# Forgetting attention and a bilinear feed-forward on one core: the first third of a literal instruction order replaced

## The chip, the core and the metric

The program runs on one NeuronCore of a Trainium2 chip. The core has a matrix engine (PE, whose weight loads are shown apart as PEld), three engines for elementwise work (DVE, ACT, POOL), and SP, which here only issues transfers. Each engine works through its own queue in order. Matrix products land in PSUM, and one of DVE or ACT has to bring them to SBUF. The metric is the device time of one execution in microseconds.

## The reference

Inputs q, k, v are [8 batches, 8 heads, 576, 64] and f is [8, 8, 576], all 32-bit floats.

```python
scores = scale * np.matmul(q, k.transpose(0, 1, 3, 2))          # scale = 1/8
cum = np.cumsum(np.log(np.clip(f, 0.0001, 1.0)), axis=-1)
decay = cum[:, :, :, None] - cum[:, :, None, :]
scores = np.where(causal, -1000000000.0, scores + decay)
attn = np.exp(scores - np.max(scores, axis=-1, keepdims=True))
attn = attn / (np.sum(attn, axis=-1, keepdims=True) + 1e-09)
x = np.matmul(attn, v)                  # then heads side by side: x is [4608, 512]
return (x @ w_a) * (x @ w_b) @ w_out    # 512 -> 1536 -> 512
```

## The kernel before

**Attention.** The 64 heads are taken in 32 pairs t = 0 to 31; four pairs make one batch (t = 4*b + pr). A pair's 576 queries are cut in five blocks i = 0 to 4 of 128 rows (the last has 64), and causality cuts the keys of each. For a block PE makes the scores from the transposed q and k (tiles `qT`, `kT`, line 550; `sc` in PSUM), DVE takes the row maximum (line 645), ACT the exponential (lines 704 and 700), DVE the reciprocal of the row sum (line 714), and POOL or ACT multiplies it in (lines 725 and 723). The weights P (tiles `PA` for blocks 0 to 2, `PB` for 3 and 4) are transposed, in the first eight pairs mostly by PE against an identity (`psP`, brought back by lines 288 to 292), later by a transposing transfer that SP issues (line 739). PE multiplies them with v (line 768, `pv` and `pvx`), and DVE writes the result, transposed, to `xT0` to `xT3`, one tile for each place of a pair in its batch. For the first two batches PE adds the decay inside the score product (`crow`, `pick`, and the causal mask by `neg`, `low`); from the third on DVE adds it from a tile `spread` that a transfer or a PE product (`scd`) fills.

**Start.** Batch 0's q and k are loaded and cast to 16 bits by transfers that POOL issues (line 333), since POOL's queue is the one that can cast; the halves beyond the first go to the space of `wout`, which is free then. POOL also builds the identity (two instructions from masks.py). PE transposes q and k against it (`psT`, line 358), and DVE or ACT evicts them to `qT` and `kT`. In the places where PE would stand idle at the start, 24 operations "wake" make products that nobody reads (line 74, tile `wake`, four matmuls each).

**Feed-forward.** It runs on token chunks of 256, 256, 256, 384, four times 512, 384, and the last 1024 tokens in a form with fewer products. Of a chunk, PE makes `psa` = x@w_a and `psb` = x@w_b for 128 columns of the 1536 at a time, ACT or DVE casts `psa` to `a` (line 288), DVE multiplies `psb` by it (line 1072, `ht`), and `pso` is the product with w_out. The matmuls of all of these go through one helper, line 74. The first chunk needs rows 0 to 255 of batch 0 in all four `xT` tiles, that is, blocks 0 and 1 of pairs 0 to 3.

**What sets the order.** The program records 2480 operations, each with a number, its engine or the engines it may run on, and what it depends on. At the end `laid_out` reads three literal texts: ORDER is the sequence of the operation numbers, in which they are then written out (each engine's queue keeps it), CHOICE gives the engine for those that have a choice (D for DVE, A for ACT, P for POOL), and SLOTS says for each buffer ring which of its places each tile takes. PSUM has a ring of two for scores (`sc`, two banks each) and a ring of four (`ff`) for everything else; f32 loads share three places (`n32`).

```python
n_of = [x.split("-") for x in ORDER.split()]
seq = [ops[n] for x in n_of for n in range(int(x[0]), int(x[-1]) + 1)]
for o in ops:
    o.eng = names[next(letters)] if len(o.durs) > 1 else next(iter(o.durs))
...
for o in order:
    o.fn(o.eng)
```

The function of the kernel is one long function, of which the changed tables and their reader are a part:

Of the kernel before, what the change touches and what calls it, by code (L numbers as in the profile page):

```python
# [25 lines left out]
def kernel(  # L26
# [13 lines left out]
    B, H, S, D = q.shape  # L40
# [22 lines left out]
    qd = [perm.tile([128, 128], FP16, tag=f"qd{i}", name=f"qd{i}") for i in range(2)]  # L63
# [41 lines left out]
    def paddings():  # L105
# [14 lines left out]
    nv = [perm.tile([128, NSB, H, D], FP16, tag=f"nv{i}", name=f"nv{i}") for i in range(2)]  # L120
# [21 lines left out]
        PA:012302310231023102310231023102310231;PB:01101010101010101010101010101010;S:0101101001101001101010110  # L142
        0110101010101001010101010101010010011010100101001000100010011011010011010100110101001101010110101010101
        ;a16:0120120120120120120120120120120121021021201201201201021021020210210120120121021021021021021;bc:012
        0120120120120120120120120120;ff:01230123013200031230120131312313102312022101012133203012301230123012301
        2301302132021021230230201230231021301230123012012302131231231021230130230132103120301010312013210321023
        1023023102310321321302130213013210321032103102132132012312312303021021023103120313201302130230123120312
        0302102012120102301310210213023123201321301321320120320312032130213021302301213021303210312303021021320
        130213201302312031203120321032102301;ht:0123456789abcd0123456789abcd0123456789ab01cd2345678a019b23cd456
        8017a29bd345c0168279a34bd015c2;n16:01101001011000101001010101010101;n32:0120102102102102010202121220120  # L150
        110102121101202201201201202120;nv:0101010101;osb:010101010100101010101010101001;qd:01010101010101010101
        0101;sc:01010101010101010101010110100101011000101010110010010101101010101011010101010101010100101011101
        10010101011001010111010101010101010101010101010101;st:01234510324510324510324510324510
# [1404 lines left out]
    for n in cuts:  # L1558
# [5 lines left out]
        0 1 29 30 46 2 52 62 5 3 31 37 32 38 33-36 39 40 42 41 53 47 58 4 43 267 262 279 6-9 54 48 10 56 50 44  # L1564
# [161 lines left out]
```

## Time and profile before

| what | value |
|---|---|
| median of three runs | 394.4 us (393.54 to 395.13) |
| profiled execution, its own time | 396.1 us |
| its span from the first to the last instruction | 394.4 us |
| mean granted PE clock | 0.999 |
| PE busy | 381.1 us, 97% of the span |
| DVE busy | 329.1 us, 83% |
| ACT busy | 299.4 us, 76% |
| POOL busy | 281.0 us, 71% |
| first feed-forward product | at 35.80 us |

The span is what one execution shows from its first instruction to its last; its own time is 1.7 us longer, which lies around the span. That the span equals the median of the three runs is chance. In rows of the timeline the first number is the start in us, the second the time that the row's instructions take together, "x16" their count; "[0.30 <-DVE kT L292]" behind a row says that the engine stood idle for 0.30 us ahead of it, and what released it. Matmuls overlap, so two rows' starts tell more of a duration than the second number does.

### The profile page before, as it was taken

How to read it: one execution, taken by the hardware profiler on the slowest of the kernel's cores; microseconds unless marked ns; L12 is line 12 of the kernel's file. 1: busy time of each engine (PE TensorE's matmuls, PEld its weight loads, DVE VectorE, ACT ScalarE, POOL GpSimd, SP SyncE). 2: the span in 40 equal slices, each digit the busy share in tenths (PEclk: the TensorE clock that was granted, in tenths of full speed). 3: DMA queues.
4: the chain of work that ended last, by engine and by line, in shares of the span. 5: the costliest groups of instructions: out<-in, count | busy, mean ns of one | idle time of the engine just before them, and what ended most of it. 6: DMA issues, size and time to landing. Idle time of an engine off the chain costs nothing.

```text
span 394.4 us, 14909 instructions
## 1 busy us (share of the span) xinstructions
PE 381.1 (97%) x5816; PEld 253.9 (64%) x5816; DVE 329.1 (83%) x1035; ACT 299.4 (76%) x826; POOL 281.0 (71%) x482
## 2 busy tenths in 40 slices
PE   7899999999998999999899999999999999999996
PEld 3557887968765665655555655555555667666796
DVE  7888898998996888788788888757898899987992
ACT  4998999999886878868888588779899672556331
POOL 8689686768867689874899769578976891267600
PEclk9999999999999999999999999999999999999999
DMA  7999999999999999999998999999998898100005
GB/s 121 251 202 170 144 154 223 228 278 275 208 222 215 220 282 247 281 187 277 260 237 255 262 207 229 206 244 263 226 226 195 169 182 178 55 1 2 2 2 214
DMA packets 147190, 76.88 MB, mean 195 GB/s; under 512 B 124336, under 2 KB 128176, under 8 KB 147120
## 3 DMA queue, kind: packets, MB, share of 16 engines
q1 hardware_dynamic: 132824, 68.79, 77.9%
q0 software_dynamic: 14256, 7.08, 14.7%
q8 instruction: 45, 0.74, 0.8%
q14 instruction: 25, 0.20, 0.2%
q10 hardware_dynamic: 40, 0.07, 0.1%
HBM read 52.05 MB, written 9.58 MB: 156 GB/s over the span
## 4 chain that ended last, share of the span: by engine, by line
PE 73%; DMA 11%; DVE 5%; POOL 4%; ACT 3%; issue 2%; ACTq 0%; DVEq 0%; POOLq 0%
PE psa L74 15%; PE psb L74 15%; PE pso L74 13%; PE wg L74 5%; DMA PTA<-PA 5%; PE wb L74 4%; PE sc L550 3%; PE og L74 3%; DMA PTB<-PB 3%; PE pvx L768 3%; PE psT L358 2%; DVE S L673 2%; DMA wb<-in_moe_w_b_dram 2%; POOL PA L725 2%; PE wake L74 2%
## 5 line engine op out<-in xcount | busy, mean ns | idle before, releaser
L673 DVE CUSTOM_DVE_ANT_0 S<-sc,spread 64x576 f32<-64x576 f32 (+4 forms) x232 | 125.5, 561 | 14.5 <-ACT PA L704 4.8
L725 POOL TENSOR_SCALAR PA<-PA,st 128x256 f16<-128x256 f16 (+2 forms) x180 | 85.0, 481 | 9.6 <-DVE st L714 6.0
L74 PE MATMUL psb<-xT,wb 128*64 128x512 f16 (+2 forms) x864 | 88.7, 332 | 0.4 <-DVE ht L1072 0.2
L704 ACT ACTIVATE PA<-S,st 128x256 f16<-128x256 f32 (+2 forms) x168 | 84.1, 503 | 6.4 <-DVE st L673 5.8
L74 PE MATMUL psa<-xT,wa 128*64 128x512 f16 (+2 forms) x864 | 88.9, 333 | 0.0
L74 PE MATMUL pso<-wout,ht 128*64 128x512 f16 x672 | 81.8, 381 | 0.0
L725 POOL TENSOR_SCALAR PB<-PB,st 128x512 f16<-128x512 f16 (+1 forms) x90 | 63.6, 713 | 25.3 <-DVE st L714 8.8
L74 PEld LDWEIGHTS <-wb 128*64 128x64 f16 x960 | 55.9, 110 | 24.9 <-issue 1.8
L74 PEld LDWEIGHTS <-wa 128*64 128x64 f16 x960 | 55.2, 110 | 24.7 <-issue 2.2
L1072 DVE TENSOR_TENSOR ht<-psb,a 128x512 f16<-128x512 f32 (+1 forms) x90 | 57.5, 648 | 7.2 <-PE psb L74 5.1
L288 ACT CAST a<-psa 128x512 f16<-128x512 f32 (+1 forms) x90 | 49.4, 550 | 18.0 <-PE psa L74 15.8
L74 PEld LDWEIGHTS <-ht 128*64 128x64 f16 x696 | 38.3, 110 | 26.8 <-issue 2.2
L704 ACT ACTIVATE PB<-S,st 128x512 f16<-128x512 f32 x56 | 40.2, 720 | 3.2 <-DVE st L673 2.7
L704 ACT ACTIVATION_READ_ACCUMULATOR PA<-S,st 128x1 f32 x168 | 32.1, 191 | 0.0
L630 POOL TENSOR_SCALAR_AFFINE_SELECT spread<-spread 128x768 f32<-128x768 f32 x24 | 20.8, 866 | 14.0 <-DMA spread<-cum_d 13.9
L700 ACT ACTIVATE PB<-S,st 128x576 f16<-128x576 f32 x28 | 21.7, 776 | 10.7 <-DMA PTB<-PB 4.1
L768 PEld LDWEIGHTS <-nv 128*64 128x64 f16 x640 | 21.8, 110 | 8.5 <-DMA PTA<-PA 2.3
L673 DVE CUSTOM_DVE_ANT_1 S<-sc,spread 128x256 f32<-128x256 f32 x48 | 19.7, 419 | 7.5 <-ACT PB L704 1.6
L1273 POOL TENSOR_TENSOR hy<-wu 128x512 f16<-128x512 f32 x9 | 11.6, 1302 | 19.7 <-DVE wu L1273 19.6
L714 DVE RECIPROCAL st<-st 128x2 f32<-128x2 f32 x128 | 18.1, 156 | 7.2 <-ACT PA L704 3.6
L673 DVE DVE_READ_ACCUMULATOR2_ANT st<- 128x1 f32 (+1 forms) x280 | 22.8, 81 | 0.0
L550 PE MATMUL sc<-kT,qT 64*128 64x512 f16 (+4 forms) x144 | 21.0, 326 | 1.2 <-ACT kT L288 0.4
(156 smaller groups left out, 692.8 us busy)
## 6 DMA issues: line engine op xcount, KB each, us to landing
spread<-cum_d SPq DMA_DIRECT2D x24, 576.0 KB, 6.4
q<-in_q_dram SPq DMA_DIRECT2D x14, 576.0 KB, 5.3
k<-in_k_dram SPq DMA_DIRECT2D x14, 576.0 KB, 5.4
out_dram<-osb SPq DMA_DIRECT2D x29, 256.0 KB, 4.0
v<-in_v_dram SPq DMA_DIRECT2D x24, 256.0 KB, 5.8
wout<-in_moe_w_out_dram POOLq DMA_DIRECT2D x3, 512.0 KB, 8.0
nv<-in_v_dram POOLq DMA_DIRECT2D x8, 128.0 KB, 5.1
wa<-in_moe_w_a_dram POOLq DMA_DIRECT2D x2, 512.0 KB, 7.5
```

What stands on the lines that cost most here:

```text
L74: nc.tensor.matmul(out=out[r], lhsT=lhsT[:, r], rhs=rhs, **kw)
L288: nc.scalar.copy(out=out_, in_=in_)
L550: nc.tensor.matmul(out=dst, lhsT=lhsT, rhs=rhs, start=start, stop=stop, skip_group_check=True)
L630: nc.gpsimd.affine_select(out=c[:, :, 0:SM].rearrange("p h (j k) -> p h j k", k=128), in_=c[:, :, SM:2 * SM].rearrange("p h (j k) -> p h j ...
L673: nc.vector.tensor_tensor_reduce(out=o, in0=x, in1=y, scale=-1.0, scalar=3e38, op0=ADD, op1=MIN, accum_out=m)
L700: nc.scalar.activation(out=p_blocks(t, 4), in_=T[("s" if direct else "z", t, 4)], func=EXP, bias=st[:, 8:9], scale=sign, accum_out=st[:, 1 ...
L704: nc.scalar.activation(out=p_blocks(t, i)[:, :, h, :], in_=(T[("s", t, i)][:, h, :] if direct else T[("z", t, i)][:, h * n:h * n + n]).rea ...
L714: nc.vector.reciprocal(out=st[:, 20 + 2 * i:22 + 2 * i], in_=st[:, 10 + 2 * i:12 + 2 * i])
L725: VEC[e].tensor_scalar(out=p, in0=p, scalar1=st[:, c:c + 1], scalar2=1.0, op0=MUL, op1=MUL)
L768: nc.tensor.matmul(out=o[HP[h], 128 * i:128 * i + 128], lhsT=vt[:, j, pr + NP * h, :], rhs=pt[:, base_blk[i] + 2 * block_at(t, i, j) + h, ...
L1072: nc.vector.tensor_tensor(out=ht[:, 0:n_], in0=T.pop(("psb", t0, fbs))[:, 0:n_], in1=T.pop(("a16", t0, fbs))[:, 0:n_], op=MUL)
L1273: VEC[e].tensor_tensor(out=out_, in0=x, in1=y, op=op)
```

## The change

Only the three texts change; the code that records the operations, and each operation, is the same. The last 1720 operations of ORDER are the same in the same sequence; the first 760 are arranged anew, and 45 operations get another engine. SLOTS is written anew to suit.

```diff
     SLOTS = """
-        PA:012302310231023102310231023102310231;PB:01101010101010101010101010101010;S:0101101001101001101010110
+        PA:012330123012301230123012301230123012;PB:01101010101010101010101010101010;S:0101010110100101100101010
...
     ORDER = """
-        0 1 29 30 46 2 52 62 5 3 31 37 32 38 33-36 39 40 42 41 53 47 58 4 43 267 262 279 6-9 54 48 10 56 50 44
+        2 5-10 519 11 12 52 53 3 0 1 29 30 13 31 32 54 37 38 55 46 47 33 34 39 62 48 58 43 56 57 36 50 49 51 35
...
     CHOICE = """
-        DDDDADADADAAPPAPPPAPPAADAPPPPPPAPADDDDPPPAPPPPPDDDDPAAPAPPPADDDADAADAAAADDPPPAPAPPPADDAAPPAPPAPAADADAAA
+        DDPDAAAADDDAPPPAPPAPPDDADPPAPPPAPPDDDDAPAPPPPPPDDDDPPAPAPPPPDDADDAAAAAAADDPPPPPPPPADDDDAPPAPAPPPDDAAPPP
```

On PE the heads that differ have the same 184 operations in another sequence; behind them, from a score product of pair 11 on (line 538, at 109.75 us in the trace of before), PE's sequence is the same. DVE gets one operation more in its head (232 for 231), POOL three more (137 for 134), ACT four fewer (173 for 177).

On PE all 24 wakes stand ahead of the first `psa` before and after. Of the work that stood ahead of it, three transposes of P (block 2 of pairs 0, 2 and 3, six matrices each) and the score products of blocks 3 and 4 of pair 2 now stand behind it, and one `scd` product from behind it stands ahead. The score products of blocks 0 and 1 of pair 2 and 3 stood behind those of block 2 of pair 0, and pair 3's also behind block 2 of pairs 1 and 2; now those of all four pairs stand ahead of the first product of a block 2. The order of SP begins with a load of the last 64 rows of batch 2's v, ahead of the load of f.

POOL from its start, before (a tile's number is its place in the program's count; `k16` and `q16` are the first halves of batch 0's k and q, `wout16` the place of the second halves):

```order
L333 DMA k16_130<-in_k_dram 64x2x576
masks.py:197 MEMSET ident16_70 128x128
masks.py:199 ISA
masks.py:199 AFFINE_SELECT ident16_70<-ident16_70 128x128
L333 DMA q16_136<-in_q_dram 64x2x576
L333 DMA wout16_78<-in_q_dram 128x2x576
L333 DMA q16_136<-in_q_dram 64x2x576
L333 DMA k16_130<-in_k_dram 64x2x576
L333 DMA wout16_78<-in_k_dram 128x2x576
```

and after:

```order
masks.py:197 MEMSET ident16_70 128x128
masks.py:199 ISA
masks.py:199 AFFINE_SELECT ident16_70<-ident16_70 128x128
L333 DMA q16_170<-in_q_dram 64x2x576 x2
L333 DMA k16_239<-in_k_dram 64x2x576 x2
L333 DMA wout16_78<-in_q_dram 128x2x576
L333 DMA wout16_78<-in_k_dram 128x2x576
```

The identity moves ahead of the first load of k, and both parts of q ahead of k.

DVE from the first row maxima on, before (`st` is a pair's small tile of maxima and sums, `sc0` holds the scores of blocks 0 and 1, `sc1` of block 2, `sc2` of block 3, `sc3` of block 4):

```order
L645 TENSOR_REDUCE st_384<-sc0_301 128x2 x2
L645 TENSOR_REDUCE st_384<-sc1_337 128x2
L290 TENSOR_SCALAR qT_253<-psT_318 128x576
L292 COPY kT_255<-psT_356 128x576
L714 RECIPROCAL st_384<-st_384 128x2
L645 TENSOR_REDUCE st_458<-sc0_403 128x2 x2
L714 RECIPROCAL st_384<-st_384 128x2
L292 COPY kT_255<-psT_421 128x576
L645 TENSOR_REDUCE st_545<-sc0_479 128x2 x2
```

and after:

```order
L645 TENSOR_REDUCE st_371<-sc0_315 128x2 x2
L645 TENSOR_REDUCE st_425<-sc0_334 128x2 x2
L290 TENSOR_SCALAR qT_268<-psT_374 128x576
L714 RECIPROCAL st_371<-st_371 128x2
L292 COPY kT_272<-psT_435 128x576
L714 RECIPROCAL st_371<-st_371 128x2
L292 COPY kT_272<-psT_436 128x576
L645 TENSOR_REDUCE st_512<-sc0_491 128x2 x2
L292 COPY spread0_84<-scd_508 128x512
L645 TENSOR_REDUCE st_554<-sc0_524 128x2 x2
```

Pair 1's first maxima now follow pair 0's at once, and pair 3's are the last row; before, pair 3's stood eight rows below the last one printed, behind two more maxima of block 2 (one of them is in the second row printed).

DVE up to the last eviction that the first `psa` needs, before:

```order
L292 CAST xT2_74<-pv_786 128x256
L645 TENSOR_REDUCE st_458<-sc2_814 128x2
L292 CAST xT0_72<-pv_737 128x256
L645 TENSOR_REDUCE st_458<-sc3_823 128x1
L292 CAST xT1_73<-pv_873 128x256
L292 COPY xT3_75<-psP_855 128x768
L292 COPY xT3_75<-psP_903 128x768
L292 CAST xT3_75<-pv_922 128x256
```

and after:

```order
L292 CAST xT0_72<-pv_708 128x256
L292 CAST xT1_73<-pv_745 128x256
L714 RECIPROCAL st_554<-st_554 128x2
L292 COPY xT3_75<-psP_726 128x768
L292 COPY spread1_85<-scd_742 128x512
L645 TENSOR_REDUCE st_371<-sc2_755 128x2
L292 CAST xT3_75<-pv_781 128x256
L714 RECIPROCAL st_425<-st_425 128x2
L714 RECIPROCAL st_371<-st_371 128x2
L645 TENSOR_REDUCE st_371<-sc3_764 128x1
L292 COPY xT2_74<-psP_801 128x768
L292 CAST xT2_74<-pv_843 128x256
```

The four casts from `pv` are the evictions in question; the last one is pair 3's before and pair 2's after, and of the larger maxima (`sc2`, `sc3`) those of pair 0 stand ahead of it now, where before those of pairs 0 and 1 did.

74 lines of the change are left out of this document (45 added, 29 removed), and 168 rows, old and new, of the table ORDER.

## The prediction

> **What bounds the kernel now.** I read the page first (span, busy times, the chain that ended last), then busy times by stage, then PE's timeline up to the first feed-forward product.
>
> ```profile
> span 394.4 us, 14909 instructions
> PE 381.1 (97%) x5816; PEld 253.9 (64%) x5816; DVE 329.1 (83%) x1035; ACT 299.4 (76%) x826; POOL 281.0 (71%) x482
> PE 73%; DMA 11%; DVE 5%; POOL 4%; ACT 3%; issue 2%; ACTq 0%; DVEq 0%; POOLq 0%
> ```
>
> PE is busy for 97% of the span and carries 73% of the chain. The same by stage (after the two times: the stretch's length, then busy time of PE, PEld, DVE, ACT, POOL, and the granted clock):
>
> ```profile
> 2.80:35.80 33.00, 30.98 (x544) 18.14 (x545) 27.90 (x68) 27.43 (x83) 27.95 (x55) 1.00 1.07 203
> 35.80:109.75 73.95, 73.59 (x1534) 60.23 (x1529) 67.34 (x237) 69.49 (x192) 56.63 (x93) 1.00 1.15 213
> 109.75:130.00 20.25, 18.28 (x266) 12.40 (x262) 16.59 (x62) 15.84 (x50) 14.84 (x28) 1.00 1.11 234
> ```
>
> 35.80 is the first feed-forward product, 109.75 the score product from which PE's sequence is the same in both orders. Between the two PE is unbusy for 0.36 us. So whatever PE work is moved from ahead of 35.80 to behind it is paid there in full, since no idle time waits to take it in. Where the 33 us ahead of the first product go:
>
> ```profile
> 2.80 4.48 PE L74 MATMUL wake<-ident 128*64 128x512 f16 x20 [2.80 <-POOL ident masks.py:199]
> 7.21 0.69 PE L358 MATMUL psT<-ident,q 64*64 64x64 f16 x18
> 7.71 0.66 PE L358 MATMUL psT<-ident,k 64*64 64x64 f16 x18
> 8.30 1.06 PE L74 MATMUL wake<-ident 128*64 128x512 f16 x8
> 9.29 0.48 PE L358 MATMUL psT<-ident,wout 64*64 64x64 f16 x36
> 9.70 0.34 PE L550 MATMUL sc<-kT,qT 64*128 64x256 f16 x4
> 20.27 0.34 PE L550 MATMUL sc<-kT,qT 64*128 64x256 f16 x4
> 32.70 0.53 PE L74 MATMUL psP<-ident,PA 128*64 128x128 f16 x12 [0.16 <-POOL PA L725]
> 33.06 0.60 PE L74 MATMUL wake<-ident 128*64 128x512 f16 x4
> 34.06 0.41 PE L74 MATMUL scd<-crow,pick 128*64 128x512 f16 x2
> 34.27 0.36 PE L768 MATMUL pv<-xT,nv 128*64 128x128 f16 x6
> 34.56 0.39 PE L550 MATMUL sc<-kT,qT 64*128 64x512 f16 x2
> 35.80 1.06 PE L74 MATMUL psa<-xT,wa 128*64 128x256 f16 x16
> 109.75 0.51 PE L538 MATMUL sc<-kT,qT 64*128 64x128 f16 x10
> ```
>
> PE starts at 2.80. Ahead of 109.75 it is unbusy for 2.80 + 2.02 + 0.36 = 5.18 us altogether, and since its set of operations there does not change, that total (and what slow matmuls at the start may give) bounds what a new order can gain by 109.75. PE looks busy, but part of it is wakes, whose products nobody reads. The useful chain is elsewhere: first scores of pair 0 at 9.70, of pair 3 only at 20.27, then maxima, exponentials, norms, transposes, and the products with v, whose evictions by DVE release 35.80. DVE, with 27.90 busy of 33.00, is the densest engine of that chain.
>
> **The change, part by part.** *1. Start.* Now the identity stands ahead of the loads in POOL's queue.
>
> ```profile
> 1.33 0.83 POOL L333 DMA_DIRECT2D k<-in_k_dram  x1 [0.81 <-POOLq L1710]
> 2.46 0.29 POOL masks.py:199 TENSOR_SCALAR_AFFINE_SELECT ident<-ident 128x128 f16<-128x128 f16 x1
> ```
>
> The load that stood ahead goes behind: 2.15 − 1.33 = 0.82 us (the next instruction began at 2.15), so the identity ends at 2.75 − 0.82 = 1.93 and PE starts at 1.98. The k load itself now stands third, behind both q loads; its transposes come late enough on PE to cover that (nine wakes stand ahead now, five before). If that cover is short, the price is one or two issues of 0.83. PE's row is then five wakes at the first row's price, 4.48; four more at 0.99 a pair (8.30 to 9.29), 2.0; four groups of transposes at 0.50 (7.21 to 7.71), 2.0; two wakes, 0.5 to 1.0. Pair 0's first scores: 1.98 + 4.48 + 2.0 + 2.0 + 0.7 = 11.2, against 9.70, thus 1.5 later. Pair 1's follow at once.
>
> The first 20 wake matmuls took 0.224 us each, the next eight 0.124 (0.99 / 8). The Trainium skill, "TensorE: Matmul & The Clock Gate", section "What's actually happening", says that the array runs at half rate until about 3.4 us of sustained activity, a span of time in a free-running window and not a number of matmuls. By that rule an earlier start ends the slow phase earlier, perhaps inside the fifth wake, an estimate of up to 0.8 us less or more at 11.2; the trace agrees that there is a slow phase and cannot show what sets its end.
>
> *2. DVE's chain to the last eviction.*
>
> ```profile
> 10.36 1.89 DVE L645 TENSOR_REDUCE st<-sc 128x2 f32<-128x512 f32 x3 [0.61 <-PE sc L550]
> 20.93 1.02 DVE L645 TENSOR_REDUCE st<-sc 128x2 f32<-128x512 f32 x2
> 17.20 0.68 DVE L292 COPY spread<-scd 128x512 f32<-128x512 f32 x1
> 25.20 0.74 DVE L292 COPY kT<-psT 128x576 f16<-128x576 f16 x1
> 25.92 1.20 DVE L645 TENSOR_REDUCE st<-sc 128x2 f32<-128x1024 f32 x1
> 27.77 1.04 DVE L292 COPY xT<-psP 128x768 f16<-128x768 f16 x2
> 34.76 0.41 DVE L292 CAST xT<-pv 128x256 f16<-128x256 f32 x1
> ```
>
> A maximum starts 0.66 behind its scores (9.70 to 10.36): 11.8 now. From there to the end of pair 3's first maxima the new order has four double maxima (1.02 each), three evictions of q or k (0.74), one copy (0.68) and two reciprocals (some 0.3): 4.1 + 2.2 + 0.7 + 0.3 = 7.3, thus 19.1, against 20.93 + 1.02 = 21.95. Behind it and up to the last of the four evictions the new order has nine reciprocals (0.8), three copies to spread (2.0), four maxima of block 2 (3.8, taken at 0.96, between the 1.02 and 1.20 of the rows shown), one kT (0.7), four copies from psP (2.1), one maximum over 1024 (1.2), one over 576 (0.7), four casts (1.6): 13.0, thus 32.1 without waits. Before, the same stretch took 35.17 − 21.95 = 13.2 with waits in it. I take 32.4 for the first psa, against 35.80: **−3.4**. Ends: −4.0 (no wait and a shorter slow phase) to −1.4 (the waits of about 2 us that DVE had there come again).
>
> *3. What PE owes.* Three transposes of P, 0.36 each (32.70 to 33.06), and the score products of blocks 3 and 4 of pair 2, 1.24 (34.56 to 35.80), go behind the first psa; one scd, 0.21 (34.06 to 34.27), comes ahead. 1.08 + 1.24 − 0.21 = **+2.1**, with PE dense up to 109.75. Nothing hides it.
>
> *4. New waits behind the first psa.* Pair 2's transpose now follows POOL's last norm of that block closely, and a transpose of batch 1's q follows POOL's cast; walking both queues I find some 0.35 and 0.25 of wait. Against that goes the wait at 45.18, since w_b's first third is issued earlier: **+0.4**, ends −0.2 and +1.5. The ends are that wait alone, and two norms late (0.59 each) with what they hold up.
>
> ```profile
> 32.06 0.59 POOL L725 TENSOR_SCALAR PA<-PA,st 128x384 f16<-128x384 f16 x1
> 45.18 1.06 PE L74 MATMUL psb<-xT,wb 128*64 128x256 f16 x16 [0.21 <-DMA wb<-in_moe_w_b_dram]
> ```
>
> *5. Changes of the array's shape.* Behind a psa group a group of another shape starts later than a like one:
>
> ```profile
> 42.10 1.04 PE L74 MATMUL psa<-xT,wa 128*64 128x256 f16 x16
> 43.07 0.44 PE L358 MATMUL psT<-ident,k 64*128 64x64 f16 x18
> 46.05 1.07 PE L74 MATMUL psa<-xT,wa 128*64 128x256 f16 x16
> ```
>
> 43.07 − 42.10 = 0.97, against 0.87 from the psb group at 45.18 to the psa group at 46.05, thus 0.10 for a change. Counted in the two orders, there are 91 changes of shape up to the common sequence before and 96 after; three of the five more lie behind the first psa: **+0.3**, ends 0 and +0.5. The Trainium skill, "TensorEngine Tiling (Array Packing)", section "Key Properties", says that a change of the tiling mode, other than one of tile, drains the array; that speaks against this order by the same 0.10 each, and the trace agrees with the sign.
>
> *Sum* at 109.75: −3.4 + 2.1 + 0.4 + 0.3 = −0.6 us. From there PE's sequence is the same and I carry the shift to the end: 394.4 − 0.6 = **393.8**. The sum is made against the profiled execution, whose span is 394.4 and own time 396.1; the 1.7 around the span do not change, and the span happens to equal the median of the runs, so I put the shift on 394.4. Own range of this case: ends of the terms taken two at a time, 392.5 to 395.4. About 0.5%, 2.0 us, is what a measurement here tells from no change (the three runs lie 1.6 apart).
>
> **The rivals.** *Faster, 391.3: the middle eases too.* Behind 109.75 PE waits for SP's transposing transfers:
>
> ```profile
> 110.86 5.22 SPq L739 DMA_TRANSPOSE PTB<-PB  x1
> 116.17 5.48 SPq L739 DMA_TRANSPOSE PTA<-PA  x2
> 122.42 0.36 PE L768 MATMUL pvx<-PTA,nv 128*64 128x128 f16 x6 [0.72 <-DMA PTA<-PA]
> 125.66 0.43 PE L74 MATMUL sc<-kT,qd 128*64 128x512 f16 x4 [1.03 <-DVE xT L292]
> ```
>
> SP's queue in the head is rearranged and several loads of batch 2 and 3 stand earlier. If the loads no longer crowd there, 0.72 + 1.03 = 1.8 us go; with terms 4 and 5 at nothing the sum is −3.4 + 2.1 − 1.8 = −3.1: 391.3. For it: PE is unbusy for 1.97 us in that stretch, the largest loss behind the start. Against it: the two issues of over 5 us come from SP's own queue behind 109.75, which is the same in both orders.
>
> *Slower, 396.8: ACT comes late and becomes the pace.*
>
> ```profile
> 7.94 0.65 ACT L286 ACTIVATE qT<-psT 128x576 f16<-128x576 f16 x1 [2.27 <-PE psT L358]
> 50.00:80.00 30.00, 30.00 (x625) 24.73 (x621) 27.63 (x104) 29.35 (x83) 23.09 (x36) 1.00 1.20 205
> ```
>
> ACT begins with four evictions as soon as transposes are there: at about 9.1 now, 7.94 before, so its first exponential comes 1.3 later; one eviction (0.65) goes to DVE, which leaves 0.7. Walking its new row I find a wait of some 1.2 ahead of pair 2's exponentials of block 2. Together 1.9 late near 50 us, where ACT has 0.65 idle of 30. If what ACT is late by sets PE's pace there, the gain at the first psa is lost and 1.9 + 0.5 (a norm behind POOL) come on top: 396.8. It decides from the point where the wait for ACT's casts of psa exceeds the three spare places of the PSUM ring. Against it: four operations fewer on ACT in the head, about 2.5 us at these durations, mostly ahead of the third chunk.
>
> *No effect, 394.4:* DVE's waits come again in full, −1.4, and cancel against 2.1 owed with half of the rest. This lies in the main case's range.
>
> **How the numbers follow.** Main case 0.46, 393.8, within 0.5%; no effect 0.06; faster rival 0.27; slower rival 0.21. Main and no effect together 0.52; of them 0.02 falls below 392.4 and 0.01 above 396.4. So faster by over 0.5% 0.29, within 0.49, slower 0.22. The range 391.0 to 396.7 takes in the main case and most of the faster one, and ends where the slower rival begins to hold half of its chance: about 0.1 is left out on each side.
>
> **What the profile after would show.** Step 1: PE's first wake at 1.98 and pair 0's scores at 11.2. Step 2: pair 3's scores near 17 instead of 20.27, the first psa at 32.4 (31.8 to 34.4). Step 3: the line-538 product at 109.2 (107.9 to 110.8), thus most of the 3.4 gone again. Step 4: a wait on POOL's PA behind the first psa, none on w_b. Slower rival: idle PE between 35 and 80 released by ACT. Faster rival: no waits over 0.5 at 120 to 126. Wrong I would be above all if DVE's stretch of 13 us runs into new waits, since then the debt of 2.1 stays without its gain.

## The result, and the profile after

The new order is slower by a little: 395.89 us median of 19 runs (392.9 to 399.61) against 394.31 of 19 runs of the order before (392.08 to 396.32), a ratio of 1.0054 with a 95% interval of 1.0027 to 1.0080. The time lies inside the forecast range, but the sign is wrong. Now and then any kernel has a slow execution, over 1.5% above its fastest one; the medians here are taken with these and the ratios without them. The profiled execution of the new order has a span of 393.5 us and took 395.17 itself, 0.7 below its median, while the one of before (396.1) lies 1.8 above its own. So the two spans, 393.5 and 394.4, say nothing on which order is faster. They serve to find out where the time moved.

The page of after, with the rows that answer to those of before:

```profile
span 393.5 us, 14916 instructions
PE 382.8 (97%) x5816; PEld 250.5 (64%) x5816; DVE 328.4 (83%) x1036; ACT 296.9 (75%) x822; POOL 281.6 (72%) x485
PE 76%; POOL 7%; DMA 7%; ACT 4%; issue 3%; DVE 2%; POOLq 0%; DVEq 0%
```

Nothing shows at this height: PE at 97% again. By stage (length, busy time of PE, PEld, DVE, ACT, POOL, granted clock, DMA share, GB/s), cut at PE's first wake, the first `psa`, and the product of pair 11 from which PE's sequence is common:

```profile
1.43:33.85 32.42, 29.60 (x492) 16.23 (x493) 26.65 (x65) 25.49 (x77) 25.30 (x53) 0.95 1.14 209
33.85:113.59 79.74, 77.78 (x1584) 62.47 (x1582) 69.56 (x241) 69.72 (x191) 59.00 (x94) 1.00 1.08 210
113.59:130.00 16.41, 16.41 (x246) 11.69 (x246) 14.93 (x59) 14.21 (x45) 15.29 (x29) 1.00 0.93 195
```

The first stage ends at 33.85, 1.95 earlier than before. The second takes 79.74 us instead of 73.95, and PE is unbusy in it for 1.96 instead of 0.36. In the third, PE has no idle time left, where it had 1.97 in 20.25. PE's timeline at the places that the prediction named:

```profile
1.43 6.77 PE L74 MATMUL wake<-ident 128*64 128x512 f16 x36 [1.43 <-POOL ident masks.py:199]
...
10.71 0.34 PE L550 MATMUL sc<-kT,qT 64*128 64x256 f16 x4
...
16.93 0.34 PE L550 MATMUL sc<-kT,qT 64*128 64x256 f16 x4
...
30.66 0.57 PE L358 MATMUL psT<-ident,q 64*128 64x64 f16 x18 [2.17 <-POOL q L290]
...
31.62 0.61 PE L550 MATMUL sc<-kT,qT 64*128 64x512 f16 x2
...
33.85 1.23 PE L74 MATMUL psa<-xT,wa 128*64 128x256 f16 x16
...
37.76 0.39 PE L550 MATMUL sc<-kT,qT 64*128 64x512 f16 x2
...
52.04 0.21 PE L358 MATMUL psT<-ident,k 64*128 64x64 f16 x2 [1.29 <-issue]
...
57.96 0.25 PE L768 MATMUL pv<-xT,nv 128*64 128x128 f16 x2 [0.26 <-issue]
...
113.59 0.51 PE L538 MATMUL sc<-kT,qT 64*128 64x128 f16 x10
```

Three things were not in the forecast: PE waits 2.17 at 30.66 for a cast of q by POOL; a like score product takes 0.61 behind that wait and 0.39 at 37.76; and PE waits at 52.04 and 57.96 with nothing recorded that releases it.

The account at the common product is 113.59 − 109.75 = +3.84 us: −1.95 at the first `psa`, +1.96 of work owed behind it, +1.60 of waits behind it (1.96 in place of 0.36), and +2.23 by which the same operations take longer between their starts.

In these profiles the rest of the program gives much of that back. The stretch from the common product to the end of the span:

```profile
109.75:394.40 284.65, 276.54 (x3750) 175.55 (x3744) 232.30 (x725) 201.77 (x554) 194.83 (x329) 1.00 0.87 191
```

```profile
113.59:393.50 279.91, 275.43 (x3746) 171.83 (x3744) 231.72 (x727) 201.65 (x554) 196.59 (x334) 1.00 0.87 191
```

The first row is before, the second after. The stretch is 4.74 shorter, and PE is unbusy in it for 8.11 before and 4.48 after. The profile of before is one of its longer executions. Measured to PE's last product instead, over the profiles before, before_again, before_ident and before_cut (the order before or nearly so) and after, after_again and after_cut, the stretch takes 281.0, 280.15, 277.9 and 277.8 before and 276.2 three times after, some 3.0 less in the mean, while the common product stands at 109.55 in the mean before and at 113.84 after, +4.3. The difference, +1.3, is near the +1.6 of the medians. But how much the tail gives back is not settled: in the variants of the new order below, whose sequence behind the common product is the same, it takes 276.0 to 279.9 (eight profiles, leaving out free_slot and q0_wakes_3, whose profiles are of their longest executions), and as after_again the new order was 1.1% longer, 4.3 us, as if nothing were given back.

Why q comes late is seen in the new order's own views. Its chain of work that ended last, around 30 us (start, us, what):

```profile
19.01 10.29 DMA q<-in_q_dram
29.45 1.16 POOL q L290
30.66 0.57 PE psT L358 x18
```

The transposes follow POOL's cast of q at once, and the cast the landing of a load that took 10.29. POOL's timeline at the cast:

```profile
29.45 1.15 POOL L290 TENSOR_SCALAR q<-q 128x1152 f16<-128x1152 f32 x1 [3.46 <-DVE st L714]
```

POOL stood idle 3.46 ahead of it. The row names DVE's reciprocal, which ended at 29.36, at nearly the same time as the load landed (29.30); where the cast comes earlier, in wakes_at_gap below, its row names the load:

```profile
28.53 1.15 POOL L290 TENSOR_SCALAR q<-q 128x1152 f16<-128x1152 f32 x1 [2.82 <-DMA q<-in_q_dram]
```

SP's queue, the loads of batch 1 and the first load of all:

```profile
0.81 0.74 SPq L299 DMA_DIRECT2D v<-in_v_dram  x1
...
9.93 0.48 SPq L338 DMA_DIRECT2D k<-in_k_dram  x1
10.45 8.94 SPq L338 DMA_DIRECT2D q<-in_q_dram  x2
...
30.63 14.96 SPq L338 DMA_DIRECT2D k<-in_k_dram  x2
```

SP issues the second of the two q loads at 19.01, where before all three first loads of batch 1 were issued by 10.8 (9.23 0.43, 9.70 0.51 and 10.26 0.52 in the rows of before). The 32-bit loads share three places. In the new order the tail of batch 2's v, the first load of SP's queue, holds one of them up to its cast by POOL at 78.67, so k and one half of q fill the other two, and the other half of q, which PE needs first, waits for the cast of k, which ended at 18.99. What PE's clock did in the two windows around the wait (columns as above):

```profile
25.00:30.00 5.00, 3.49 (x64) 2.01 (x58) 4.88 (x13) 4.33 (x13) 1.51 (x4) 1.00 1.25 194
30.00:35.00 5.00, 4.34 (x62) 2.85 (x64) 2.31 (x7) 3.36 (x8) 4.97 (x9) 0.66 0.94 212
```

and, cut to where the clock changed:

```profile
30.81:34.22 3.41, 3.41 (x46) 1.93 (x42) 1.84 (x5) 2.55 (x6) 3.38 (x6) 0.50 0.91 226
```

The granted clock fell to 0.50 for 3.41 us, 0.66 over the 5 us behind a gap of 2.17 us; in before the same window has 1.00. Half of 3.41 is 1.7 us of PE's work, and 0.004 of an execution's mean clock. The Trainium skill, "TensorE: Matmul & The Clock Gate", section "HAM oscillation — how this bites in real kernels", gives the rule as no idle gaps of PE over about 3.4 us. Here a gap of 2.2 was enough, and the measurement decides. The free-running window of that page (section "What's actually happening") would explain why it does not happen in every execution, which no run here shows. Of the 19 executions of the new order, 11 had a mean granted clock of 0.996 or less, and their median was 397.5 against 395.5 of the other eight. Of the 110 of the order before that ran beside the experiments below, five had. An execution without a profile tells only that its clock fell, not where.

The waits that "issue" released are PE's own program being loaded. The page's list of DMA queues (packets, MB, share of the time of the 16 engines) names one queue for it:

```profile
q8 instruction: 45, 0.74, 0.8%
```

PE executes some 11,600 instructions, matmuls and weight loads, and 45 loads of 256 instructions (0.74 MB in all, 16 KB each) make that. The two waits stand 256 PE instructions apart (the 1722nd and the 1978th), that is, at borders of blocks. In the traces one such load starts behind nearly each border that PE crosses, up to 5.4 us later; by the waits it brings the block behind the one that PE has just entered. For the wait at 52.04 PE entered the block before at 45.4; the load started 4.3 later at 49.7, took 1.0, and PE went on 1.35 behind its landing. That makes 6.6 us, and the block itself held only 5.3 of work: the wait is the difference. In the 4.2 us between, the listing of queues has no instruction transfer at all, and this row for the transfers that POOL issued:

```profile
q0 software_dynamic: 612, 0.61, 105.1%
```

They alone take 105% of the 16 engines' time, so the transfers in flight had a backlog. In the order before the same load started 1.6 behind its border, at 44.7, landed at 45.7 and was needed at 49.5. The backlog alone does not explain the difference, though: from 41 to 57 us POOL's transfers take more of the engines' time in the order before (first row) than in the new one (second row).

```profile
q0 software_dynamic: 5460, 2.34, 124.6%
```

```profile
q0 software_dynamic: 3543, 1.84, 92.5%
```

And at the next border of the order before the load started 3.1 late, with POOL's transfers at 110%, and PE did not wait, since the block held 5.8 of work. The Trainium skill, "Runtime: NRT & Kernel Launch", section "Instruction fetch mechanics", says the same of the size, 256 instructions, and that crossing a border is mostly hidden. The trace agrees on the size; here the crossing cost up to 2.2 us.

### The profile page after: what moved, and what is told of

Read it like the earlier page. It is cut to its first block, busy times and chain, and to the rows that moved or that the text cites. A ratio compares the mean times of both kernels' runs of the same rounds, so it can differ in the third digit from the quotient of the medians.

```text
span 393.5 us, 14916 instructions
## 1 busy us (share of the span) xinstructions
PE 382.8 (97%) x5816; PEld 250.5 (64%) x5816; DVE 328.4 (83%) x1036; ACT 296.9 (75%) x822; POOL 281.6 (72%) x485
## 4 chain that ended last, share of the span: by engine, by line
PE 76%; POOL 7%; DMA 7%; ACT 4%; issue 3%; DVE 2%; POOLq 0%; DVEq 0%
PE pso L74 16%; PE psb L74 16%; PE psa L74 16%; PE wg L74 4%; PE sc L550 4%; DMA PTA<-PA 4%; PE pvx L768 3%; PE wb L74 3%; PE og L74 3%; DMA q<-in_q_dram 3%; PE psT L358 2%; PE sc L538 2%; PE psP L74 2%; POOL PA L725 1%; ACT PA L704 1%
## 5 line engine op out<-in xcount | busy, mean ns | idle before, releaser
L725 POOL TENSOR_SCALAR PB<-PB,st 128x512 f16<-128x512 f16 (+1 forms) x92 | 64.9, 713 | 26.8 <-DVE st L714 11.6
L74 PEld LDWEIGHTS <-wb 128*64 128x64 f16 x960 | 55.0, 110 | 25.4 <-issue 1.8
L74 PEld LDWEIGHTS <-wa 128*64 128x64 f16 x960 | 54.3, 110 | 25.6 <-issue 2.2
L290 POOL TENSOR_SCALAR q<-q 128x1152 f16<-128x1152 f32 x14 | 16.1, 1150 | 8.0 <-DVE st L714 5.8
```

The lines of the kernel that those rows point to most:

```text
L74: nc.tensor.matmul(out=out[r], lhsT=lhsT[:, r], rhs=rhs, **kw)
L290: VEC[e].tensor_scalar(out=out_, in0=in_, scalar1=0.125, scalar2=1.0, op0=MUL, op1=MUL)
L725: VEC[e].tensor_scalar(out=p, in0=p, scalar1=st[:, c:c + 1], scalar2=1.0, op0=MUL, op1=MUL)
```

## The experiments

Theory A: the late load of q, with the slow clock behind it, makes the order slower. Theory B: the head itself owes more than it gains (work moved behind the first `psa`, changes of shape, waits for code). Rival C: a shift of the head is carried to the end 1:1. Edits of ORDER are shown as the piece that changes; places in SLOTS follow suit. Each ratio is against the order before, run beside it on the same chip.

**free_slot**: the tail of batch 2's v goes back behind the other loads of v, so that it no longer holds a place at the start.

```diff
-  2 5-10 519 11 12 52 ...   ... 1758 520 383 ...
+  2 5-12 52 ...   ... 521 517 519 385 ... 509 518 520 511 ...
```

> The new order with one thing undone: the load of batch 2's last rows of v (and its cast) goes back behind the other v loads of that batch, so that it holds none of the three places for f32 loads during the start. Theory A (the place held by that load delays batch 1's q, and POOL's cast of it makes PE wait 2.17 us at 30.66, lose its full rate behind, and wait 1.29 us once more at 50.35): the load of q is issued near 11 us instead of 19.01, the wait of 2.17 goes, the granted clock of 30 to 35 us is 1.00, and the score product of pair 11 that begins the common sequence, at 113.59 in the profile of the new order, comes at 108.3 to 110. Rival B (POOL's and ACT's new rows are late by themselves, and the load only happens to come last): another wait takes the place, and that product stays behind 111.8. On the end: if a shift of the head is carried to the end, the time falls by 3.5 to 5 us against the new order (391 to 392.5); if waits behind the head take a shift in, it falls by 1 to 2 us (394 to 395).

400.7 us, 1.0139 (1.0086 to 1.0192). PE's wait for q was gone; waits of 0.56 and 0.83 for DVE's evictions stood in its place. But the renumbered places made another load wait. SP's timeline of this kernel (the profile is of its longest execution, 405.79):

```profile
81.25 1.56 SPq L624 DMA_DIRECT2D spread<-cum_d  x1
89.43 1.00 SPq L299 DMA_DIRECT2D v<-in_v_dram  x2
```

Batch 3's v waited for its place at the head of SP's queue and held it from 82.81 to 89.43, 6.6 us; it was issued at 79.78 in after. POOL then stood idle 5.32 at 101.1, and the common product came at 120.24. The first `psa` was no earlier than in after, 34.56: a wait with no recorded releaser, 1.44, stood ahead of 15.27, and the clock was 0.50 for the 3.41 us behind 16.79. This run tells A and B apart only as far as the wait for q goes.

**q0_first**: the two q loads change places, the half that PE needs first now being loaded first.

```diff
-  121 279 225 232 ... 103 267 268 257
+  121 267 225 232 ... 103 279 268 257
```

> The new order with batch 1's loads of q's first half and second half exchanged in SP's queue, nothing else: the first half is issued second, the second half waits for the place. The load of v keeps its place. Theory A: the first half lands before 22 us, the 2.17 us wait of PE is gone, the second half comes in time for its cast at 44 us; the product of pair 11 comes at 109 to 111. Rival B: the same wait for POOL or another stays, the product behind 111.8. End as for the run before: 391.5 to 393 if carried, 394 to 395.3 if taken in.

396.24 us, 1.0040 (1.0003 to 1.0077). The first `psa` came at 31.98, 1.87 earlier than in after, and the common product at 111.86. The long wait is replaced by two, 0.55 and 0.83, on DVE's evictions, and in 7 of 12 executions the mean clock was still 0.996 or less (their median 397.0, of the other five 394.5).

**wakes_at_gap**: three wakes that stand ahead are moved to the place of the wait, the loads left as they are.

```diff
-  144 26 265 ... 173 27 135 ... 234 28 248 ... 105 269 211
+  144 265 ... 173 135 ... 234 248 ... 105 26 27 28 269 211
```

> The new order with the last three of the 24 wakes moved to directly ahead of the transposes of batch 1's q, where PE waits 2.17 us; data and loads as before, so the wait for the cast stays and is only filled (three wakes are 1.3 us). If the slow matmuls from 30.66 to 35 us come from PE's idle time, they run at the full rate now (0.22 instead of 0.40 us per two score matmuls) and the product of pair 11 comes 1.5 to 2 us earlier than 113.59 in a profile that would have the slow phase; if they come from contention with transfers, they stay slow. End: 0.5 to 1.5 us below the new order (394.4 to 395.4) if the slow phase is one of the causes, 395.9 if not.

396.84 us, 1.0063 (1.0031 to 1.0095). The first `psa` came at 32.64, the common product at 112.38, and 2 of 12 executions had the low clock. The same window as above, of this kernel, with the gap filled:

```profile
30.00:35.00 5.00, 4.94 (x112) 3.81 (x108) 2.89 (x8) 4.34 (x11) 4.89 (x8) 1.00 1.06 222
```

POOL's cast of q was at 28.53 here, 0.92 earlier than in after, and PE still stood idle for 0.78 ahead of the moved wakes; the rest of the gap they filled. So the clock followed the gap: with q still late and wakes in the gap, the clock stays at 1.00. The time is still longer than before, so the clock is not the whole of it.

**q0_wakes**: q0_first with one wake ahead of each of the two short waits.

```diff
-  173 27 135 ... 234 28 248 ... 105 269 211
+  173 135 ... 234 248 ... 105 27 269 28 211
```

> The run q0_first with two of the last three wakes moved into PE's waits of 0.55 and 0.83 us ahead of the first psa (ahead of the transposes of batch 1's q and ahead of pair 2's product with v). If idle time of PE there is what lowers the granted clock in about half of the executions (7 of 12 of q0_first at 0.996 or less, 11 of 19 of the new order, 1 of 23 of before), at most 3 of 12 are low now and the median falls from 1.3 us above before to 0 (within 0.7). If the low clock comes from elsewhere, the share stays near half.

393.24 us, 1.0001 (0.9971 to 1.0031); the first `psa` at 32.16, the common product at 112.28. Run again as **q0_wakes_2** on the chip of the runs of after_again below:

> The run q0_wakes once more, beside the new order on one chip: the load of q in time, and two wakes in the waits. If the late load and the clock are the whole loss, the ratio to before is 0.997 to 1.002 again and 0.4% or more under the new order's. If the first result was the chip's, it is above 1.004.

396.14 us, 1.0060 (1.0025 to 1.0094); common product 112.07. And a third time as **q0_wakes_3**:

> The run q0_wakes, unchanged, as the base of q0_wakes_cut on one chip: 0 to 0.6% above before, the two waits in its profile.

396.08 us, 1.0057 (1.0025 to 1.0089). The first reading, which had the order level with before, didn't come again. The first two readings are of one chip, so two readings of one kernel's ratio can lie 0.6% apart, as much as an interval is wide. With the late load gone the common product stays at 112.07 to 112.28, some 2.6 behind the 109.55 of the order before; that part is B's.

**after_again** is the new order unchanged, and **wakes_2** is wakes_at_gap again, both beside q0_wakes_2 on one chip.

> The new order, unchanged, on the same chip as the three runs beside it, for a fair comparison. Near 1.005 of before, low granted clock (0.996 or less) in about half of its executions; the profile shows the wait for POOL's cast of batch 1's q again (1.5 to 2.5 us) if it belongs to the order.

> The run wakes_at_gap once more, beside the new order on one chip. If the low clock is the cost: few low executions and a ratio 0.2 to 0.4% under the new order's. If the gap itself is the cost and not the clock: the new order's ratio within 0.1%, with few low executions.

after_again: 398.17 us, 1.0108 (1.0066 to 1.0149). wakes_2: 397.44, 1.0081 (1.0048 to 1.0114). On one chip, then, the order cost 1.1%, without the slow clock 0.8%, and without the late load 0.6%. That has A at up to half of it, but the intervals overlap, and the same pair with its wakes cut (after_cut and q0_wakes_cut below) shows no gain, so what A costs in time is not shown. That A is not the whole is shown better: without the late load the order was still slower in every reading but the first of q0_wakes. PE's timeline of after_again shows how the wait at the border of a block varies:

```profile
29.44 0.43 PE L358 MATMUL psT<-ident,q 64*128 64x64 f16 x18 [1.35 <-POOL q L290]
...
56.96 0.25 PE L768 MATMUL pv<-xT,nv 128*64 128x128 f16 x2 [2.18 <-issue]
```

```profile
55.00:65.00 10.00, 8.04 (x134) 5.44 (x135) 6.54 (x23) 6.11 (x18) 5.24 (x9) 0.83 0.81 93
```

The wait for q was 1.35 here and the score products behind it took their usual 0.39; the wait for code was 2.18, and the clock fell behind that one, to 0.83 over 10 us (0.50 from 58.13 to 61.54). The low clock cost less here than in after: the four executions that had it have a median of 398.4, the other two 397.95. The first `psa` was early, 31.65, and the common product late, 114.95.

**q0_k1**: q0_wakes, and POOL's cast of a half of k moved ahead of a norm, to try whether the wait near 50 is for that cast.

```diff
-  238 201 202 297 ... 244 275
+  238 201 275 202 297 ... 244
```

> The run q0_wakes with POOL's cast of batch 1's second half of k ahead of one norm, without the moved operations of PE that went along with it in q0_all. The wait of 0.96 to 1.29 us at the transposes of that k (48 to 50 us) goes; pair 11's product at 111.0 to 111.6 instead of 112.28. If it is carried: 0.2% under q0_wakes, below before. Rival, as q0_all showed: a norm or an eviction is late instead, the product stays at 112 or later, and the time is q0_wakes' or above.

396.97 us, 1.0055 (1.0019 to 1.0092). The cast ended at 44.9 and the wait stayed, 1.02 at 50.41. It is not the cast.

**q0_all**: q0_k1, and three PE operations moved by one to five places, so that the shape changes to and from 64 rows behind the first `psa` go from 39 to 33.

```diff
-  168 169 125 126 293 ... 170 171 ... 1720 ... 348 1721 1722 ... 455 524 522
+  168 169 125 126 170 1721 293 ... 171 ... 1720 ... 348 1722 ... 499 524 382 ... 455 522
```

> The run q0_wakes with two things more: POOL's cast of batch 1's second half of k one place earlier, ahead of a norm for which POOL waits 1.49 us (PE waits 0.96 for that cast at 48.39), and three operations of PE moved by a few places behind the first psa, so that it changes between 64-row groups and others 33 times up to pair 11's product instead of 39 (before: 31). By the price of 0.09 us a change found from the four traces, that is 0.5 us; the wait gives up to 0.9. Pair 11's product comes at 110.0 to 110.8 instead of 111.86. At the end: 393.5 to 394.5 if it is carried, as q0_wakes if taken in at 122 to 126. Rival: the small waits move on to other operations and the product stays behind 111.3.

399.01 us, 1.0156 (1.0098 to 1.0214), with the common product at 116.33. PE's timeline has waits that q0_k1 and after do not have there:

```profile
79.23 0.29 PE L538 MATMUL sc<-kT,qT 64*128 64x128 f16 x4 [0.97 <-ACT kT L288]
...
82.78 1.06 PE L74 MATMUL psb<-xT,wb 128*64 128x256 f16 x16 [0.73 <-ACT a L288]
...
84.70 0.35 PE L783 MATMUL pv<-PTB,nv 128*64 128x64 f16 x10 [0.85 <-DVE ht L1072]
```

What six fewer changes of shape gained is lost several times over to ACT and DVE arriving late. The price of a change of shape is therefore known only from the traces, not from this run.

**after_cut, q0_wakes_cut, before_cut**: each wake product is cut in two halves of the same columns, which puts 192 PE instructions more (96 products and their weight loads) ahead of everything, and shifts all borders of blocks.

```diff
-            mm_halves(x, ident16, ident16[:, 0:1].to_broadcast([128, 512]), start=True, ...)
+            for c in (0, 256):
+                mm_halves(x[:, c:c + 256], ident16, ident16[:, 0:1].to_broadcast([128, 256]), start=True, ...)
```

> The new order with each dummy product of the 24 wakes cut in two of 256 columns: the same time on the array, 192 instructions of PE more, all ahead of the first psa. Code theory: the waits at the second transposes of batch 1's k (near 50 us, 0.65 to 1.97 in five profiles) and at pair 2's product with v (near 57, 0.26 to 2.18) are gone from these operations, since the borders of 256 instructions now lie 192 instructions earlier in the work, near 46 and 52 us; waits without a visible releaser are found there or nowhere. Rival: the two waits stay at the same operations, since a cast, an eviction or a PSUM place sets them. Time: within 0.5% of the new order's either way.

> The run q0_wakes with its wakes cut in the same way. Code theory: the waits of 1.06 to 1.26 and 0.54 to 0.81 us at these two operations go; if none takes their place, pair 11's product comes at 110.3 to 110.8 instead of 112.1 to 112.3 and the time falls by 1 to 1.8 us, to before or below. Rival: waits and time stay as in q0_wakes.

> The kernel before with its wakes cut in the same way. Code theory: a wait with no releaser can come up at one of the new borders (near 39.8, 45.3, 50.5 us, with 5.2 to 5.5 us from border to border in two of them); if it does, the time rises by 0.5 to 1.5 us. If the loads are in time, as in the order before, it is the same within 0.3%. Rival (such waits belong to the operations of the new order): no wait without a releaser anywhere.

after_cut: 396.96 us, 1.0062 (1.0028 to 1.0096). q0_wakes_cut: 396.76, 1.0078 (1.0050 to 1.0107). before_cut: 393.94, 1.0014 (0.9985 to 1.0043). From PE's timeline of after_cut:

```profile
50.53 0.43 PE L359 MATMUL psT<-ident,k 64*128 64x64 f16 x18
...
52.86 0.53 PE L74 MATMUL psP<-ident,PB 128*64 128x128 f16 x12 [0.52 <-issue]
...
58.23 0.30 PE L74 MATMUL psP<-ident,PB 128*64 128x128 f16 x4 [0.22 <-issue]
```

The transpose of k that waited at 52.04 no longer waits; the wait is on another operation, at the new border. And before_cut got such a wait, which its order had never shown:

```profile
40.37 0.29 PE L551 MATMUL sc<-neg,low 64*128 64x64 f16 x8 [1.37 <-issue]
```

So it belongs to the place in the program and not to the operation: it is the loading of code. Shifting the borders did not do away with it: after_cut also had waits of 0.74 ahead of 13.13 and of 1.64 inside the wakes, ahead of 19.82, and q0_wakes_cut had 0.88 ahead of 18.64 and 1.32 ahead of 58.15. A late block somewhere is what these heads pay; in the order before each block up to 107 us landed 1.8 to 7.4 us before PE needed it.

**before_ident**: the order before, with the load of k behind the identity alone.

```diff
-  0 1 29 30 46 2 52
+  0 1 29 30 2 46 52
```

> The kernel before with one part of the change alone: the identity ahead of the first load of k in POOL's queue. PE's first wake comes at 1.4 to 2.0 instead of 2.80. If the start is what counts, pair 0's scores come 0.5 to 0.8 earlier than 9.70, and the first psa and pair 11's product keep it (35.1, 109.1). Taken-in theory: the waits at 122 to 126 grow by the same 0.6, and the time is that of before within 0.3 us. Carried theory: 0.6 us less at the end. Rival: batch 0's loads land no earlier, the transposes wait for q's landing (6.62), and nothing changes from 9.70 on.

393.46 us, 1.0008 (0.9975 to 1.0040). Its PE timeline:

```profile
1.43 3.97 PE L74 MATMUL wake<-ident 128*64 128x512 f16 x20 [1.43 <-POOL ident masks.py:199]
6.24 0.47 PE L358 MATMUL psT<-ident,q 64*64 64x64 f16 x18 [0.84 <-DMA q<-in_q_dram]
...
8.90 0.48 PE L358 MATMUL psT<-ident,wout 64*64 64x64 f16 x36 [0.93 <-DMA wout<-in_q_dram]
9.31 0.34 PE L550 MATMUL sc<-kT,qT 64*128 64x256 f16 x4
```

PE starts 1.37 earlier and gives 0.98 of it back waiting for loads; pair 0's scores come 0.39 earlier, the first `psa` 0.18 (35.62), the common product 0.36 (109.39). This step of the change alone is worth nothing that can be measured.

**delay4** and **before_again**: for rival C, the order before with 19 products that nobody reads added in pair 11's scores (`t == 11`, at the common product; 4.24 us from their start to the next product in its trace), and the order before unchanged.

```diff
+        if t == 11:
+            for _ in range(19):
+                mm_halves(c[:, 0, :], ident16, ident16[:, 0:1].to_broadcast([128, 512]), start=True, ...)
```

> The kernel before with 4.1 us of additional dummy products (19 times two matmuls of 512 columns) on PE in front of pair 11's first score product, the point from which PE's sequence is common; they are computed and overwritten. If a shift of PE there is carried to the end: 394.3 + 4.1 = 398.4. If the waits of PE behind that point (0.72 and 1.03 us at 122 to 126, and smaller ones to 325) take it in, as the new order's profile suggests (3.84 us late there, 0.94 early at the end): 394.5 to 396.5.

> The kernel before, unchanged, for a second profile of it. If PE's waits of 0.72 and 1.03 us at 122 to 126 belong to the kernel, they stand there again (1.5 to 2 us between 118 and 130); the waits of 1.1 us near 188 and of 0.46 and 0.65 at 264 and 325 then show whether they are the one execution's or the kernel's. If all of them move, the tail's waits are chance and nothing can be said to take a shift in.

delay4: 401.84 us, 1.0200 (1.0142 to 1.0258), that is 7.9 us (5.6 to 10.2) for 4.24 added; its lines count 4 more. The added products are 76 PE instructions with their weight loads, so the borders of blocks behind them shift as well. PE was 3.5 late behind the added work and only 1.2 late at 130, since the waits between 118 and 130 went. Then others came. PE's waits of delay4 behind 130 (in total, times, longest):

```profile
PE psa L74 <- ACT a L288: 2.0, 1, 2.0
PE pvx L772 <- DMA PTA<-PA: 1.3, 1, 1.3
PE sc L542 <- DVE ht L1076: 1.0, 1, 1.0
```

The last of the three, at 191.1, is one that the order before has too (1.15 at 188.4); the other two are new or longer. Its span is 400.0, 5.6 longer for 4.24 added. So a delay at the common product was not taken in. before_again, of one execution (394.76), has a span of 393.0, with waits of 0.4 and 0.2 us where its order had 1.03 in the profile shown ahead, so these waits vary from one execution to another; the wait of `sc` for DVE's `ht`, 1.1 near 188, is in it as in the other profiles of this order and in none of the new one.

## Where the prediction was right and where it was wrong

The sum was −3.4 + 2.1 + 0.4 + 0.3 = −0.6 and came out as −1.95 + 1.96 + 1.60 + 2.23 = +3.84. What failed is step 4, which had waits on POOL and none on code, step 5, which had the wrong count of changes, and the part of step 2 that left out the loads; the work owed was right. These figures are of one profile of each order.

**Step 1, the start: right, and half a microsecond short.** PE's first wake at 1.43 (1.98 forecast), pair 0's scores at 10.71 (11.2), with a wait of 0.33 for the load of k at 9.31 all the same. before_ident shows the covering that the step assumed: without nine wakes in front, PE waits for the loads.

**Step 2, DVE's chain: right in mechanism, with a wait missing.** Pair 3's scores came at 16.93, "near 17" as forecast. The first `psa` came at 33.85 instead of 32.4, since PE itself waited 2.17 for q and then ran at a low clock. Where that was lessened it came at 31.65 (after_again), 31.98 (q0_first), 32.16 (q0_wakes) and 32.64 (wakes_at_gap), thus about where DVE's chain had been put. In free_slot and after_cut, with waits for code ahead of it, it came at 34.56 and 34.11. What failed is that I walked POOL's and DVE's queues, and of SP's order looked only at which load stood early, not at which buffer place each load holds and for how long. The wait on POOL's cast of q, which I put behind the first `psa` at 0.25, stood ahead of it at 2.17. The row that I read for DVE as the densest engine, 27.90, has POOL at 27.95.

**Step 3, the work owed: right.** 0.34 + 0.34 + 0.46 for the three transposes, 1.23 for the scores of pair 2, less 0.41 for the `scd`: +1.96, forecast +2.1.

**Step 4, the waits behind the first psa: wrong in size and in kind.** +1.60 against +0.4. The two waits with no recorded releaser, 1.29 and 0.26, make 1.55 of the 1.96 us in which PE is unbusy there; they are the loading of code. A trace of before that has no such wait gives no row for its price; the 16 KB loads were in it, landing 1.8 to 7.4 us ahead of their use, and I did not look at that slack.

**Step 5, the same operations longer: mis-sized, +2.23 against +0.3.** The price of 0.10 was right and the count was not. Two places of before, where the same product is followed once by its own shape (64*128) and once by another (64*64), show the price:

```profile
17.64 0.24 PE L550 MATMUL sc<-neg,low 64*128 64x64 f16 x4
17.69 0.44 PE L358 MATMUL psT<-ident,q 64*128 64x64 f16 x18
...
35.01 0.22 PE L550 MATMUL sc<-neg,low 64*128 64x64 f16 x4
35.16 0.43 PE L550 MATMUL sc<-kT,qT 64*64 64x512 f16 x4
```

0.05 and 0.15. Over four traces (before, before_again, after, after_again) a change between any two of the shapes that the rows print, 128*64, 64*128 and 64*64, costs 0.09 to 0.10 us, and like behind like nothing. By these shapes there are 67 changes before up to the common product and 76 after, where the forecast had 91 and 96, and what counts is where: ahead of the first `psa` 30 before and 27 after, behind it 37 and 49. Twelve more at 0.096 are +1.15. The slow clock reaches into the first group (1.06 instead of 0.90 from the first `psa` to the next start), +0.16, and around the three waits some 0.4 is lost beside their recorded length, by estimate from the starts in the rows. The rest, some 0.5, was not taken apart.

**The sum and its carrying: wrong twice, in opposite senses.** At the common product +3.84 instead of −0.6; and it was not carried to the end 1:1 in the profiles shown, where the tail gave some 3.0 back. delay4 shows that a late PE first meets fewer waits, and can then meet later ones of its own: it paid its delay in full and more. So lateness alone is not shown to shorten the tail; nor is it within the new order's variants, where wakes_2, 0.8 later than after at the common product, has a tail 3.7 longer. What does shorten it, the other sequence of transfers or chance, is open.

**The rivals.** The slower one had the sign and nearly the time (396.8), with the wrong mechanism: PE's only wait for ACT between the first `psa` and the common product is 0.18. The faster one's waits at 122 and 126 did go, as it said, but delay4 shows that a late PE alone makes them go; and the second of the two, 1.03, was by its row for DVE's eviction and not for a transfer. "Wrong I would be above all if DVE's stretch of 13 us runs into new waits" named the right thing, an early gain that is eaten while the debt stays, and the wrong engine: SP's places.

Left open: why blocks of code start to load later in the new order, since the backlog of transfers between 41 and 57 us is larger in the order before. No kernel did away with the waits for code, so what they cost in time is read from the traces alone. The other engines of 45 operations and the new SLOTS were not tried apart from the sequence. No order tried here beat the one before.

## What to carry to other kernels

Where an order of instructions is changed, walk the buffer places too: a load issued early holds its place until the operation that frees it, and a ring of three with one place held is a ring of two. A stretch that is 99% busy on its bound engine can only pay for work moved into it, so a gain ahead of it has to exceed that work and everything that the new sequence adds, changes of shape and code loads among it. And a shift in the middle says little of the end while other engines still have waits to give back or to add; look at the last product of the bound engine, over several profiles, before a sum is believed to half a percent.

## What the runs showed of the hardware

- A gap of 2.2 us on PE could lower the granted clock: to 0.50 for 3.41 us, 0.66 over 5 us behind one of 2.17 (after) and 0.83 over 10 us behind one of 2.18 (after_again). A gap of 1.44 was followed by 0.50 over 3.41 us once (free_slot, at 16.79); behind one of 1.35 (after_again) score products took 0.39 as ever, and behind one of 1.98 (delay4, at 323.7) the clock stayed at 1.00. So the length of the gap alone doesn't decide. The price was some 2 us in the 19 runs of after (397.5 against 395.5) and some 0.5 in the six of after_again.
- PE's program arrives in blocks of 256 instructions, one load behind each border that PE crosses. Where the load started 3.6 to 5.4 us behind the border (after, after_again), PE waited 0.26 to 2.18 us at the next one, and it went on 1.3 to 1.45 us behind the landing; with 3.1 us and 5.8 us of work in the block (before) it did not wait. The place of the wait moves with the count of instructions ahead of it.
- A change between the array's shapes 128*64, 64*128 and 64*64 cost 0.09 to 0.10 us, in each of the pairs, over four traces.
